# Batch 0's k sums from matmuls of their own, and its kv by head pair, in a fused attention and GEGLU kernel

## Chip, cores, metric

One core of a Trainium2 chip. The metric is the device time of one execution in microseconds (us). The profile gives a span, which runs from the first to the last instruction that it counts and is mostly 1.8 us shorter than the time. Engines: PE is TensorE, DVE is VectorE, ACT is ScalarE, POOL is GpSimd, SP is SyncE.

## The reference

```python
q_s = exp(q - max(q, -1)); q_s /= sum(q_s, -1)        # per token, over head_dim
k_s = exp(k - max(k, 2));  k_s /= sum(k_s, 2)         # per channel, over the sequence
kv  = einsum('bhsd,bhse->bhde', k_s, v)
x   = einsum('bhsd,bhde->bhse', q_s, kv)              # 8 batches, 8 heads, 576 tokens, 64 wide
out = (gelu(x @ w_gate) * (x @ w_val)) @ w_out        # x as [4608, 512]; d_ff = 1536
```

The kernel doesn't divide exp(k) by its sums; it divides kv by them, since the sum over the sequence is a factor of each row of kv.

## The kernel before

The FFN of all batches fills PE from 16 us on. The change touches what comes ahead of it for batch 0. The parts concerned, with cuts marked:

```python
def kv_mm(b, g, j):                       # one head pair; column D of v16 holds ones
    ...
    for n in range(NC):
        nc.tensor.matmul(st[(b, "pskv", g)][:, j, :], ek_b[b % 2][:, n, hp * P:(hp + 1) * P],
                         v16_b[b % 2][:, n, 2 * hp:2 * hp + 2, 0:VW], ...)     # VW = 65, N = 130

def kv_norm(b, g):                        # two head pairs
    nc.vector.reciprocal(out=rck, in_=pskv[:, :, D])
    for j in range(2):
        nc.vector.scalar_tensor_tensor(out=kv_sb, in0=pskv[:, j, ...], scalar=rck[:, j:j + 1], in1=mask, ...)

# the start, batch 0
norm_pair(0, 1, 1, ("dve", "pool")); evac_t0("dve")
warm_pe(11)
cast_v(0, 0, 2, "dve"); cast_v(0, 2, 4, "act"); cast_v(0, 6, 8, "dve"); cast_v(0, 4, 6, "act")
...                                       # loads of batches 1 and 2
kv_mm(0, 0, 0); kv_mm(0, 0, 1); kv_norm(0, 0)
unit_t(0, 1, "dve")                       # eight transposes of q and their copy
kv_mm(0, 1, 1)
unit_x(0, 0, "act", True)                 # x matmul of pair 0, copied by ACT to xt
kv_mm(0, 1, 0)
unit_x(0, 1, "act", True)
kv_norm(0, 1)
...
# first FFN block (two tiles together), x of pairs 2 and 3 in it
go(0, (0, 1)); xs(); go(1, (0, 1)); go(0, (2,)); go(1, (2,)); ...
```

Names in the profile's lines: ek and eq are exp(k) and exp(q), pskv is the product kv as PE writes it and kv_sb its normalised copy, pst are the transposes of eq and eqt their copy, psx the x matmuls and xt their copy, psg and psv the gate and value matmuls of the FFN, ht their product, psy the matmuls with w_out, pswarm the filler matmuls of PE (warm_pe), whose result isn't used. pks are the k sums.

The softmax here doesn't subtract the row's maximum and nothing guards it: scores larger than these inputs give would overflow.

Of the kernel before, what the change touches and what calls it, by code (L numbers as in the profile page):

```python
# [9 lines left out]
f32 = mybir.dt.float32  # L10
f16 = mybir.dt.float16
ACTF = mybir.ActivationFunctionType
ALU = mybir.AluOpType
# [5 lines left out]
def kernel(  # L19
# [10 lines left out]
    nc = tc.nc  # L30

    B, H, S, D = q.shape
    C = H * D
    F = moe_w_gate.shape[1]
    P = 128
    HP = H // 2
# [6 lines left out]
    NC = NM + 1  # L43
    MAIN = NM * P
    REM = S - MAIN
    VW = D + 1
# [4 lines left out]
    const = ctx.enter_context(tc.tile_pool(name="const", bufs=1))  # L51
    wpool = ctx.enter_context(tc.tile_pool(name="wpool", bufs=1))
    wstp = ctx.enter_context(tc.tile_pool(name="wstp", bufs=6))
    att = ctx.enter_context(tc.tile_pool(name="att", bufs=2))
# [3 lines left out]
    ps_big = ctx.enter_context(tc.tile_pool(name="ps_big", bufs=6, space=bass.MemoryType.PSUM))  # L58
    ps_att = ctx.enter_context(tc.tile_pool(name="ps_att", bufs=2, space=bass.MemoryType.PSUM))
# [4 lines left out]
    warm = const.tile([P, 512], f16)  # L64
    ident = const.tile([P, P], f16)
    mask = const.tile([P, 2, D], f32)
    tiny = const.tile([P, 80], f32)
    ek_b, eq_b, v16_b = [], [], []
    for i in range(2):
        ek_b.append(const.tile([P, NC, C], f16, name=f"ek{i}"))  # L70
# [9 lines left out]
    nc.vector.memset(ld_b["k"][0][:, :, 0:D], -1e30)  # L80
    nc.vector.memset(ld_b["v"][0][:, :, 0:D], 0.0)
    nc.vector.memset(tiny, 0.0)
    nc.vector.memset(mask, 0.0)
    nc.vector.memset(mask[0:64, 0, :], 1.0)
    nc.vector.memset(mask[64:128, 1, :], 1.0)
# [67 lines left out]
    def cast_v(b, h0, h1, eng="pool"):  # L153
        if eng == "pool" and h1 - h0 > 2:
            for h in range(h0, h1, 2):
                cast_v(b, h, h + 2)
            return
        copy_on(eng, v16_b[b % 2][:, :, h0:h1, 0:D].rearrange("p n h d -> p h n d"),
                tiles[("v", b)][:, h0:h1, :].rearrange("p h (n d) -> p h n d", d=D))
# [45 lines left out]

    def kv_mm(b, g, j):
        if (b, "pskv", g) not in st:
            pool, tag = (ps_big, "mm") if (b, g) == (0, 1) else (ps_att, "att")
            st[(b, "pskv", g)] = pool.tile([P, 2, 2 * VW], f32, name="pskv", tag=tag)
        hp = 2 * g + j  # L210
        for n in range(NC):
            nc.tensor.matmul(  # L212
                st[(b, "pskv", g)][:, j, :], ek_b[b % 2][:, n, hp * P:(hp + 1) * P],
                v16_b[b % 2][:, n, 2 * hp:2 * hp + 2, 0:VW],
                start=(n == 0), stop=(n == NC - 1))

    def kv_norm(b, g):
        pskv = st[(b, "pskv", g)]
        rck = att.tile([P, 2], f32, name="rck", tag="rck")
        nc.vector.reciprocal(out=rck, in_=pskv[:, :, D])  # L220
        for j in range(2):
            kv_sb = att.tile([P, 2, D], f16, name="kv_sb", tag="kv", bufs=12)
            nc.vector.scalar_tensor_tensor(
                out=kv_sb,
                in0=pskv[:, j, :].rearrange("p (h e) -> p h e", e=VW)[:, :, 0:D],
                scalar=rck[:, j:j + 1], in1=mask, op0=ALU.mult, op1=ALU.mult)
            st[(b, "kv", 2 * g + j)] = kv_sb

    def unit_kv(b, g):
        kv_mm(b, g, 0)  # L230
# [9 lines left out]
    def unit_t(b, g, eng="dve"):  # L240
        eqt = get_eqt(b)
        pst = ps_att.tile([P, 2, MAIN], f16, name="pst", tag="att")
        for j in range(2):
            hp = 2 * g + j
            for n in range(NM):
                nc.tensor.transpose(  # L246
                    pst[:, j, n * P:(n + 1) * P],
                    eq_b[b % 2][:, n + 1, hp * P:(hp + 1) * P], ident)
        st["evac_t"] = lambda eng: copy_on(eng, eqt[:, 2 * g:2 * g + 2, 0:MAIN], pst)
        if eng:  # L250
            st["evac_t"](eng)
# [49 lines left out]
    def unit_x(b, hp, eng="act", big=False):  # L301
        xt = get_xt(b)
        psx = (ps_big if big else ps_att).tile([P, MAIN], f32, name="psx",
                                               tag="mm" if big else "att")
        nc.tensor.matmul(psx, st[(b, "kv", hp)].rearrange("p h e -> p (h e)"),  # L305
                         xq(b, hp), start=True, stop=True)
        copy_on(eng, xt[:, hp, :], psx)
# [10 lines left out]
    def warm_pe(n):  # L318
        ps = pswarm
        for _ in range(n):  # L320
            nc.tensor.matmul(ps, ident, warm, start=True, stop=True)  # L321
# [5 lines left out]
    def mm_gv(ps, w, xt, fi, cis):  # L327
        for ci in cis:
            nc.tensor.matmul(ps, w[:, ci, fi * P:(fi + 1) * P], xt[:, ci, :],  # L329
                             start=(ci == 0), stop=(ci == HP - 1))  # L330
# [16 lines left out]
    def ffn_first(xt, after, between):  # L347

        ps = []
        for fi in range(len(after)):  # L350
            psg = ps_big.tile([P, 512], f32, name="psg", tag="mm")
            psv = ps_big.tile([P, 512], f32, name="psv", tag="mm")
            if fi == 0:
                for ci in range(2):
                    mm_gv(psg, wg_sb, xt, fi, [ci])
                    mm_gv(psv, wv_sb, xt, fi, [ci])
            else:
                mm_gv(psg, wg_sb, xt, fi, range(0, 2))
                for f in between[fi]:
                    f()  # L360
                mm_gv(psv, wv_sb, xt, fi, range(0, 2))
            ps.append((psg, psv))
            for f in after[fi]:
                f()
        for fi, (psg, psv) in enumerate(ps):
            mm_gv(psg, wg_sb, xt, fi, [2])
            mm_gv(psv, wv_sb, xt, fi, [2])
        hts = []
        for fi, (psg, psv) in enumerate(ps):
            mm_gv(psg, wg_sb, xt, fi, [3])  # L370
            mm_gv(psv, wv_sb, xt, fi, [3])
            hts.append(gate(psg, psv))
        return hts

    def ffn_first0(xt, xs):

        ps = {}
        for fi in range(2):
            for nm in ("g", "v"):
                ps[(nm, fi)] = ps_big.tile([P, 512], f32, name="ps" + nm, tag="mm")  # L380

        def go(fi, cis):
            for ci in cis:
                mm_gv(ps[("g", fi)], wg_sb, xt, fi, [ci])
                mm_gv(ps[("v", fi)], wv_sb, xt, fi, [ci])

        go(0, (0, 1))
        xs()
        go(1, (0, 1))
        go(0, (2,))  # L390
        go(1, (2,))
        hts = []
        for fi in range(2):
            go(fi, (3,))
            hts.append(gate(ps[("g", fi)], ps[("v", fi)]))
        return hts
# [85 lines left out]
    evac_t0 = st["evac_t"]  # L482
    norm_pair(0, 1, 1, ("dve", "pool"))
    evac_t0("dve")
    warm_pe(11)
    cast_v(0, 0, 2, "dve")
    cast_v(0, 2, 4, "act")
    cast_v(0, 6, 8, "dve")
    cast_v(0, 4, 6, "act")
    for h0 in (0, 4):  # L490
        load(k, "k", 1, h0, h0 + 4, 0)
        load(v, "v", 1, h0, h0 + 4, 0)
    load_batch(2, ((q, "q"), (k, "k")))
    nc.sync.dma_start(out=q0r, in_=q[0].rearrange("h (m n) d -> m h (n d)", n=NT)[:, :, 0:D])
    kv_mm(0, 0, 0)
    kv_mm(0, 0, 1)
    kv_norm(0, 0)
    unit_t(0, 1, "dve")
    kv_mm(0, 1, 1)
    cast_w("wg", 0, "pool")  # L500
    cast_w("wv", 0, "pool")
    unit_x(0, 0, "act", True)
    kv_mm(0, 1, 0)
    unit_x(0, 1, "act", True)
    kv_norm(0, 1)
    preload(ACTF.Gelu)
    for c in range(1, NW):
        cast_w("wg", c)
# [22 lines left out]
    first1 = ([[L(unit_kv, 1, 1), L(unit_t, 1, 1)], [], [L(unit_x, 1, 3, "dve")]],  # L531
              [[], [], [L(unit_x, 1, 2, "act")]])

    def x_upper():
        unit_x(0, 2, "dve")
        unit_x(0, 3, "act")


    at(1, FI, 2, L(unit_trem, 1))
# [52 lines left out]
    for b in order:  # L592
        xt = get_xt(b) if b < B else xtr
        hts = []
        fi0 = 0
        if b < 2:
            hts = ffn_first0(xt, x_upper) if b == 0 else ffn_first(xt, *first1)
            fi0 = len(hts)
            ride(b, FI, fi0 - 1)
        for fi in range(fi0, NFI):  # L600
            hts.append(ffn_fi(xt, fi))
            ride(b, FI, fi)
        if b == 0:
            psys = []
            for ns in range(4):
                psys.append(ps_big.tile([P, C], f32, name="psy", tag="mm"))
                mm_out(psys[ns], hts, ns, range(0, NFI // 2))
                ride(b, NS, ns)
            for ns in range(4):
                cut = 10 if ns == 3 else NFI  # L610
                mm_out(psys[ns], hts, ns, range(NFI // 2, cut))
                ride(b, NS, 14 + ns)
                mm_out(psys[ns], hts, ns, range(cut, NFI))
                evac(b, ns, psys[ns], "act" if ns == 3 else "dve")
                ride(b, NS, 4 + ns)
        else:
            for ns in range(4):
                if b == order[-1] and ns == 3:
                    last_rows(b, hts, ns)
                    break  # L620
                psy = ps_big.tile([P, C], f32, name="psy", tag="mm")
                mm_out(psy, hts, ns, range(NFI // 2))
                ride(b, NS, 10 + ns)
                mm_out(psy, hts, ns, range(NFI // 2, NFI))
                evac(b, ns, psy)
                ride(b, NS, ns)
# [30 lines left out]
```

## Time and profile before

| what | before |
|---|---|
| time, median of 3 runs (lowest to highest) | 319.98 us (319.97 to 320.21) |
| span of the profiled run | 318.5 us |
| PE busy | 98% |
| first psg (first useful FFN matmul) | 15.96 us |
| first psg of the third FFN tile | 19.91 us |

From the third FFN tile on, the FFN's own matmuls follow each other without a break that the change touches, so **the start of the third tile** is the mark that I use for the start. Its line in the timeline of the kernel before (columns: start us, duration us, engine, line, operation, output<-inputs, count):

```profile
19.91 1.03 PE L329 MATMUL psg<-xt,wg_sb 128*128 128x512 f16 x4
```

### The profile page before, as it was taken

How to read it: one execution, taken by the hardware profiler on the slowest of the kernel's cores; microseconds unless marked ns; L12 is line 12 of the kernel's file. 1: busy time of each engine (PE TensorE's matmuls, PEld its weight loads, DVE VectorE, ACT ScalarE, POOL GpSimd, SP SyncE). 2: the span in 40 equal slices, each digit the busy share in tenths (PEclk: the TensorE clock that was granted, in tenths of full speed). 3: DMA queues.
4: the chain of work that ended last, by engine and by line, in shares of the span. 5: the costliest groups of instructions: out<-in, count | busy, mean ns of one | idle time of the engine just before them, and what ended most of it. 6: DMA issues, size and time to landing. Idle time of an engine off the chain costs nothing.

```text
span 318.5 us, 4464 instructions
## 1 busy us (share of the span) xinstructions
PE 312.0 (98%) x1645; PEld 148.9 (47%) x1645; DVE 194.7 (61%) x341; ACT 139.7 (44%) x179; POOL 44.8 (14%) x59
## 2 busy tenths in 40 slices
PE   8899999999999999999999999999999999999995
PEld 3444454445445444544444444444444444444444
DVE  3944386698898469847784679457952434233331
ACT  3653565989433663256433753384331233113300
POOL 2657551330003000110003000300000000000000
PEclk9999999999999999999999999999999999999999
DMA  6999999940196117811592139303011110040002
GB/s 232 372 383 395 400 388 385 393 156 0 68 313 241 44 66 246 297 52 66 167 363 66 53 117 385 94 15 132 0 54 32 74 60 0 20 108 6 0 35 99
DMA packets 42342, 50.76 MB, mean 159 GB/s; under 512 B 3408, under 2 KB 38096, under 8 KB 42320
## 3 DMA queue, kind: packets, MB, share of 16 engines
q1 hardware_dynamic: 40592, 48.84, 44.2%
q10 hardware_dynamic: 1728, 1.64, 1.6%
q8 instruction: 13, 0.21, 0.3%
q14 instruction: 9, 0.07, 0.1%
HBM read 37.75 MB, written 9.44 MB: 148 GB/s over the span
## 4 chain that ended last, share of the span: by engine, by line
PE 88%; DMA 4%; ACT 3%; DVE 2%; issue 1%; POOL 0%; ACTq 0%; DVEq 0%; POOLq 0%
PE psy L403 28%; PE psg L329 26%; PE psv L329 26%; PE pskv L212 3%; DMA out_dram<-yo 2%; PE psx L305 2%; DMA qt<-in_q_dram 2%; PE psl L424 1%; PE pswarm L321 1%; DVE rq L165 1%; DVE ht L336 1%; ACT eq L148 1%; PE pst L246 1%; ACT xt L128 1%; POOL eq L184 0%
## 5 line engine op out<-in xcount | busy, mean ns | idle before, releaser
L334 ACT ACTIVATE gl<-psg 128x512 f32<-128x512 f32 x108 | 63.9, 598 | 128.5 <-PE psg L329 125.5
L336 DVE SCALAR_TENSOR_TENSOR ht<-psv,gl 128x512 f16<-128x512 f32 x108 | 72.9, 682 | 63.6 <-PE psv L329 63.0
L329 PE MATMUL psg<-xt,wg_sb 128*128 128x512 f16 x384 | 100.6, 379 | 0.3 <-ACT xt L128 0.2
L329 PE MATMUL psv<-xt,wv_sb 128*128 128x512 f16 x384 | 100.7, 379 | 0.0
L403 PE MATMUL psy<-wo_sb,ht 128*128 128x512 f16 x420 | 95.6, 379 | 0.0
L329 PEld LDWEIGHTS <-wv_sb 128*128 128x128 f16 x432 | 42.2, 98 | 51.8 <-issue 1.0
L329 PEld LDWEIGHTS <-wg_sb 128*128 128x128 f16 x432 | 41.5, 98 | 47.1 <-issue 0.4
L403 PEld LDWEIGHTS <-ht 128*128 128x128 f16 x420 | 40.5, 98 | 47.1 <-DVE ht L336 0.2
L452 DVE TENSOR_SCALAR yo<-psy 128x512 f32<-128x512 f32 x30 | 20.6, 689 | 31.2 <-PE psy L403 31.2
L126 POOL CAST v<-vt 128x640 f16<-128x640 f32 x26 | 18.8, 763 | 138.9 <-DMA vt<-in_v_dram 100.4
L165 DVE TENSOR_REDUCE rq<-eq 128x10 f32<-128x640 f16 x28 | 22.7, 812 | 5.1 <-ACT eq L148 4.6
L184 DVE TENSOR_TENSOR eq<-eq,rrq 128x640 f16<-128x640 f16 (+1 forms) x29 | 23.6, 815 | 0.3
L148 ACT ACTIVATE ek<-kt 128x1280 f16<-128x1280 f32 (+1 forms) x11 | 19.1, 1746 | 3.5 <-DMA kt<-in_k_dram 3.4
L148 ACT ACTIVATE eq<-qt 128x2560 f16<-128x2560 f32 (+2 forms) x10 | 18.4, 1863 | 2.3 <-DMA qt<-in_q_dram 2.3
L271 DVE STREAM_TRANSPOSE et<-eq 128x640 f16<-128x640 f16 x20 | 16.9, 846 | 0.7
L128 ACT CAST xt<-psx 128x512 f16<-128x512 f32 x17 | 9.3, 587 | 13.8 <-PE psx L305 13.8
L329 PE MATMUL psg<-xtr,wg_sb 128*128 128x512 f16 x48 | 12.3, 379 | 0.0
L329 PE MATMUL psv<-xtr,wv_sb 128*128 128x512 f16 x48 | 12.3, 379 | 0.0
L212 PEld LDWEIGHTS <-ek 128*128 128x128 f16 x160 | 10.5, 97 | 3.4
L212 PE MATMUL pskv<-v,ek 128*128 128x130 f16 x160 | 12.0, 220 | 0.0
L321 PE MATMUL pswarm<-warm,ident 128*128 128x512 f16 x41 | 10.6, 420 | 1.4 <-POOL ident masks.py:199 1.4
L130 DVE CAST xt<-psx 128x512 f16<-128x512 f32 x15 | 9.7, 682 | 2.1 <-PE psx L305 2.1
(60 smaller groups left out, 129.3 us busy)
## 6 DMA issues: line engine op xcount, KB each, us to landing
out_dram<-yo SPq DMA_DIRECT2D x14, 512.0 KB, 3.3
kt<-in_k_dram SPq DMA_DIRECT2D x7, 640.0 KB, 7.8
vt<-in_v_dram SPq DMA_DIRECT2D x7, 640.0 KB, 8.1
qt<-in_q_dram SPq DMA_DIRECT2D x7, 640.0 KB, 5.2
qt<-in_q_dram SPq DMA_DIRECT2D x8, 512.0 KB, 5.9
eqt<-et SPq DMA_DIRECT2D x80, 40.0 KB, 1.9
wost<-in_moe_w_out_dram SPq DMA_DIRECT2D x6, 512.0 KB, 7.9
kt<-in_k_dram SPq DMA_DIRECT2D x6, 512.0 KB, 7.9
```

The lines of the kernel that those rows point to most:

```text
L126: nc.gpsimd.tensor_copy(out=dst, in_=src)
L148: nc.scalar.activation(out=dst[:, n0:NC, h0 * D:h1 * D].rearrange("p n (h d) -> p h n d", d=D), in_=tiles[(nm, b)][:, h0:h1, n0 * D:NC * D ...
L165: nc.vector.reduce_sum(rq, e, axis=mybir.AxisListType.X)
L184: (nc.gpsimd if eng == "pool" else nc.vector).tensor_tensor(out=e, in0=e, in1=rrq.unsqueeze(-1).to_broadcast((P, n, 2, D)), op=ALU.mult)
L212: nc.tensor.matmul(st[(b, "pskv", g)][:, j, :], ek_b[b % 2][:, n, hp * P:(hp + 1) * P], v16_b[b % 2][:, n, 2 * hp:2 * hp + 2, 0:VW], start ...
L271: nc.vector.transpose(out=et[:, :, hp].rearrange("p c (n i) -> p n c i", i=32), in_=eq_b[b % 2][:, :, hp * P:(hp + 1) * P].rearrange("p n ...
L321: nc.tensor.matmul(ps, ident, warm, start=True, stop=True)
L329: nc.tensor.matmul(ps, w[:, ci, fi * P:(fi + 1) * P], xt[:, ci, :], start=(ci == 0), stop=(ci == HP - 1))
L334: nc.scalar.activation(out=gl, in_=psg, func=ACTF.Gelu)
L336: nc.vector.scalar_tensor_tensor(out=ht, in0=psv, scalar=_H_SCALE, in1=gl, op0=ALU.mult, op1=ALU.mult)
L403: nc.tensor.matmul(psy, hts[fi][:, ns * P:(ns + 1) * P], wo_sb[:, fi, :], start=(fi == 0), stop=(fi == NFI - 1))
L452: nc.vector.tensor_scalar(out=yo, in0=psy, scalar1=1.0 / _H_SCALE, scalar2=None, op0=ALU.mult)
```

## The change

The intent: let the sums of exp(k) be ready before v arrives, so that the reciprocal is off the chain from v to the first FFN matmul; let pair 0 go on without pair 1; and take PE's filler matmuls out of the way. The diff:

```diff
--- before.py
+++ after.py
@@ -64,7 +64,8 @@
     warm = const.tile([P, 512], f16)
     ident = const.tile([P, P], f16)
     mask = const.tile([P, 2, D], f32)
-    tiny = const.tile([P, 80], f32)
+    ones = const.tile([P, 1], f16)
+    tiny = const.tile([P, 72], f32)
     ek_b, eq_b, v16_b = [], [], []
     for i in range(2):
         ek_b.append(const.tile([P, NC, C], f16, name=f"ek{i}"))
@@ -80,6 +81,7 @@
     nc.vector.memset(ld_b["k"][0][:, :, 0:D], -1e30)
     nc.vector.memset(ld_b["v"][0][:, :, 0:D], 0.0)
     nc.vector.memset(tiny, 0.0)
+    nc.vector.memset(ones, 1.0)
     nc.vector.memset(mask, 0.0)
     nc.vector.memset(mask[0:64, 0, :], 1.0)
     nc.vector.memset(mask[64:128, 1, :], 1.0)
@@ -205,8 +207,7 @@
 
     def kv_mm(b, g, j):
         if (b, "pskv", g) not in st:
-            pool, tag = (ps_big, "mm") if (b, g) == (0, 1) else (ps_att, "att")
-            st[(b, "pskv", g)] = pool.tile([P, 2, 2 * VW], f32, name="pskv", tag=tag)
+            st[(b, "pskv", g)] = ps_att.tile([P, 2, 2 * VW], f32, name="pskv", tag="att")
         hp = 2 * g + j
         for n in range(NC):
             nc.tensor.matmul(
@@ -225,6 +226,34 @@
                 in0=pskv[:, j, :].rearrange("p (h e) -> p h e", e=VW)[:, :, 0:D],
                 scalar=rck[:, j:j + 1], in1=mask, op0=ALU.mult, op1=ALU.mult)
             st[(b, "kv", 2 * g + j)] = kv_sb
+
+
+    def ksum_mm(hps):
+        if "pks" not in st:
+            st["pks"] = ps_big.tile([P, HP], f32, name="pks", tag="mm")
+        for hp in hps:
+            for n in range(NC):
+                nc.tensor.matmul(st["pks"][:, hp:hp + 1], ek_b[0][:, n, hp * P:(hp + 1) * P], ones,
+                                 start=(n == 0), stop=(n == NC - 1))
+
+    def ksum_rec():
+        st["rck0"] = att.tile([P, HP], f32, name="rck0", tag="rck0", bufs=1)
+        nc.vector.reciprocal(out=st["rck0"], in_=st["pks"])
+
+    def kv0_mm(hp):
+        pool, tag = (ps_att, "att") if hp == 0 else (ps_big, "mm")
+        st[("pskv0", hp)] = pool.tile([P, P], f32, name="pskv0", tag=tag)
+        for n in range(NC):
+            nc.tensor.matmul(
+                st[("pskv0", hp)], ek_b[0][:, n, hp * P:(hp + 1) * P],
+                v16_b[0][:, n, 2 * hp:2 * hp + 2, 0:D], start=(n == 0), stop=(n == NC - 1))
+
+    def kv0_norm(hp):
+        kv_sb = att.tile([P, 2, D], f16, name="kv_sb", tag="kv", bufs=12)
+        nc.vector.scalar_tensor_tensor(
+            out=kv_sb, in0=st[("pskv0", hp)].rearrange("p (h e) -> p h e", e=D),
+            scalar=st["rck0"][:, hp:hp + 1], in1=mask, op0=ALU.mult, op1=ALU.mult)
+        st[(0, "kv", hp)] = kv_sb
 
     def unit_kv(b, g):
         kv_mm(b, g, 0)
@@ -385,8 +414,12 @@
                 mm_gv(ps[("v", fi)], wv_sb, xt, fi, [ci])
 
         go(0, (0, 1))
-        xs()
-        go(1, (0, 1))
+        xs[0]()
+        for ci in range(2):
+            mm_gv(ps[("g", 1)], wg_sb, xt, 1, [ci])
+        xs[1]()
+        for ci in range(2):
+            mm_gv(ps[("v", 1)], wv_sb, xt, 1, [ci])
         go(0, (2,))
         go(1, (2,))
         hts = []
@@ -482,27 +515,31 @@
     evac_t0 = st["evac_t"]
     norm_pair(0, 1, 1, ("dve", "pool"))
     evac_t0("dve")
-    warm_pe(11)
+    warm_pe(2)
+    ksum_mm((0, 1))
+    warm_pe(2)
+    ksum_mm((2, 3))
     cast_v(0, 0, 2, "dve")
     cast_v(0, 2, 4, "act")
+    ksum_rec()
+    cast_v(0, 4, 6, "act")
+    kv0_mm(0)
+    kv0_mm(1)
+    kv0_norm(0)
+    kv0_norm(1)
     cast_v(0, 6, 8, "dve")
-    cast_v(0, 4, 6, "act")
     for h0 in (0, 4):
         load(k, "k", 1, h0, h0 + 4, 0)
         load(v, "v", 1, h0, h0 + 4, 0)
     load_batch(2, ((q, "q"), (k, "k")))
     nc.sync.dma_start(out=q0r, in_=q[0].rearrange("h (m n) d -> m h (n d)", n=NT)[:, :, 0:D])
-    kv_mm(0, 0, 0)
-    kv_mm(0, 0, 1)
-    kv_norm(0, 0)
-    unit_t(0, 1, "dve")
-    kv_mm(0, 1, 1)
     cast_w("wg", 0, "pool")
     cast_w("wv", 0, "pool")
     unit_x(0, 0, "act", True)
-    kv_mm(0, 1, 0)
+    kv0_mm(2)
     unit_x(0, 1, "act", True)
-    kv_norm(0, 1)
+    kv0_norm(2)
+    unit_t(0, 1, "dve")
     preload(ACTF.Gelu)
     for c in range(1, NW):
         cast_w("wg", c)
@@ -531,9 +568,10 @@
     first1 = ([[L(unit_kv, 1, 1), L(unit_t, 1, 1)], [], [L(unit_x, 1, 3, "dve")]],
               [[], [], [L(unit_x, 1, 2, "act")]])
 
-    def x_upper():
+    def x_upper0():
+        kv0_mm(3)
+        kv0_norm(3)
         unit_x(0, 2, "dve")
-        unit_x(0, 3, "act")
 
 
     at(1, FI, 2, L(unit_trem, 1))
@@ -594,7 +632,7 @@
         hts = []
         fi0 = 0
         if b < 2:
-            hts = ffn_first0(xt, x_upper) if b == 0 else ffn_first(xt, *first1)
+            hts = ffn_first0(xt, (x_upper0, L(unit_x, 0, 3, "act"))) if b == 0 else ffn_first(xt, *first1)
             fi0 = len(hts)
             ride(b, FI, fi0 - 1)
         for fi in range(fi0, NFI):
```

## The prediction

> **What bounds the kernel now.** I read the page's busy row and tenths first, then the waits of TensorE (PE), then the timeline of the first 20 us, because the diff touches only batch 0's start.
>
> ```profile
> PE 312.0 (98%) x1645; PEld 148.9 (47%) x1645; DVE 194.7 (61%) x341; ACT 139.7 (44%) x179; POOL 44.8 (14%) x59
> ```
>
> PE is busy 98% of 318.5 us. The waits of PE over the whole execution are only these four:
>
> ```profile
> PE pswarm L321 <- POOL ident masks.py:199: 1.4, 1, 1.4
> PE pst L246 <- DVE eq L184: 0.7, 1, 0.7
> PE pst L246 <- POOL eq L184: 0.4, 1, 0.4
> PE psg L329 <- ACT xt L128: 0.2, 1, 0.2
> ```
>
> All lie before 16.0 us. From there PE has a full queue, so the end is the moment of the first useful FFN matmul plus the PE work after it. But "busy" before 16 us is partly filler (pswarm), and the chain there runs through other engines. The timeline (start us, duration us, engine, line):
>
> ```profile
> 10.12 2.43 ACT L148 ACTIVATE ek<-kt 128x1280 f16<-128x1280 f32 x2 [1.51 <-DMA kt<-in_k_dram]
> ...
> 11.13 2.54 PE L321 MATMUL pswarm<-warm,ident 128*128 128x512 f16 x11
> ...
> 12.66 1.36 ACT L128 CAST v<-vt 128x640 f16<-128x640 f32 x2
> 12.68 1.05 DVE L130 CAST v<-vt 128x640 f16<-128x640 f32 x2
> ...
> 13.51 0.74 PE L212 MATMUL pskv<-v,ek 128*128 128x130 f16 x10
> ...
> 14.08 0.61 PE L246 MATMUL pst<-ident,eq 128*128 128x128 f16 x8
> 14.28 0.17 DVE L220 RECIPROCAL rck<-pskv 128x2 f32<-128x2 f32 x1 [0.55 <-PE pskv L212]
> 14.49 0.61 DVE L223 SCALAR_TENSOR_TENSOR kv_sb<-pskv,rck,mask 128x128 f16<-128x128 f32 x2
> ...
> 14.90 0.39 PE L305 MATMUL psx<-eqt,kv_sb 128*128 128x512 f16 x1
> ...
> 15.32 1.09 ACT L128 CAST xt<-psx 128x512 f16<-128x512 f32 x2 [1.30 <-PE psx L305]
> ...
> 15.96 0.38 PE L329 MATMUL psg<-xt,wg_sb 128*128 128x512 f16 x1 [0.17 <-ACT xt L128]
> ```
>
> The reader should see one thread: v cast, kv matmuls, reciprocal, normalisation, x matmul, x copy, first psg at 15.96. The eleven warm matmuls end issuing at 13.51 (11 x 0.216 = 2.38 after 11.13), while the first v cast is done by about 13.25: PE itself holds kv up by 0.25. Then ten kv matmuls are waited for as one, and the reciprocal sits on the path.
>
> **What the Trainium skill says.** "TensorE: Matmul & The Clock Gate", Back-to-back issue gap, gives N/2.4 + 2.5 ns warm. The trace agrees: eleven N=512 matmuls at 0.216 us each, and N=130 ones at 0.057 (0.57 of the chain for ten). The same section puts a floor of 25 ns under a small N, or 62 ns if the sequencer decodes. No N=1 matmul is in this trace; since each of the 20 new ones brings its own 128-column weight load, and such pairs go at 0.057 here, I take 0.057. The same page, The HAM clock gate, says the PE clock halves after about 3.4 us of idling. The trace shows the start of it: the first warm weight loads stand 0.43 us apart, those after 4.30 us 0.21; idling of 0.66 and 0.43 before the transposes didn't bring the slow rate back. "PSUM — Partial Sum Buffer", The four PSUM rules, says a first matmul of a group clears the flags of its whole bank, so groups of one bank must not be open together: the four k sums of one bank run one after the other, so the result should be right.
>
> **The change, part by part.** Removed: seven warm matmuls (11 become 4), one of two reciprocals, the ones column of each kv matmul (N 130 to 128, 20 x under 1 ns: nothing). Added: 20 k-sum matmuls of N=1 (20 x 0.057 = 1.14 us of PE) in the time the filler had. PE there was idle in truth, so neither is worth anything by itself. Moved: kv of pair 2 between the two x matmuls; the second transposes behind them; kv of pair 3 and its normalisation behind the first four FFN matmuls; the two upper x matmuls into the first FFN block; DVE's cast of heads 6-7 behind two normalisations. ACT, POOL and SP keep their order.
>
> I work out the new times from durations above. Three latencies come from start-to-start gaps before: normalisation to the x matmul 14.90 - 14.49 = 0.41 (its own duration, 0.35, plus 0.05); x matmul to ACT copy 15.32 - 14.90 = 0.42; copy to psg 15.96 - 15.32 = 0.64. A matmul's result is seen about 0.26 after its start (last of ten kv at 14.02, reciprocal at 14.28).
>
> 1. ek's second half ends 12.55, so the last ten k sums run 12.60 to 13.17 and the reciprocal (DVE) about 13.37 to 13.54, right after DVE's only v cast before it, whose heads 0-1 are ready at 13.29.
> 2. kv of pair 0: 13.29, five at 0.057, last at 13.52, seen 13.78. Normalisation at 13.78 instead of 14.49; it no longer waits for pair 1 nor for its own reciprocal.
> 3. x of pair 0: 13.78 + 0.41 = 14.19 instead of 14.90. ACT copies it at 14.61; first psg possible at 15.25.
> 4. kv of pair 1: 13.57 to 13.86, seen 14.06; normalised, usable 14.46. kv of pair 2 14.40 to 14.69, then x of pair 1 at 14.69, its copy at 15.13 (behind the first, 0.52 apart) and usable 15.77.
> 5. The eight transposes take PE from 14.90 to 15.35, past 15.25: **first psg at 15.35**, 0.61 earlier than 15.96. The xt of pair 1 at 15.77 fits the third matmul.
> 6. From there PE has, up to its third FFN tile: 16 FFN matmuls (16 x 0.2155 = 3.45), two x (0.43) and, new, kv of pair 3 (0.28): 4.16, so 15.35 + 4.16 = 19.51. Before: 15.96 + 3.45 + 0.43 = 19.84, and 0.07 of gap made it 19.91. Check of the new waits: pair 3's kv is seen at 16.70, normalised, usable 17.10 and wanted at 17.14; DVE's xt of pair 2 runs after that, 16.96 to 17.65, wanted at 17.79. Both fit by less than 0.1.
>
> Sum: 0.61 - 0.28 + 0.07 = **0.40 us** earlier, 319.98 - 0.40 = 319.58, so I say **319.6 us**. The number of PE matmuls after that point is the same, and none is shortened.
>
> **Rivals.** (a) The gain is lost later to the DMA queue, since the loads of the weights and of batch 1 keep their times. For it: until 58 us the queue moves some 390 GB/s and other engines wait on it:
>
> ```profile
> 38.57 1.04 POOL L126 CAST wo_sb<-wost 128x1024 f16<-128x1024 f32 x1 [3.25 <-DMA wost<-in_moe_w_out_dram]
> ...
> 41.15 1.57 POOL L126 CAST wo_sb<-wost 128x1024 f16<-128x1024 f32 x1 [0.21 <-DMA wost<-in_moe_w_out_dram]
> ...
> 47.29 1.39 POOL L126 CAST v<-vt 128x640 f16<-128x640 f32 x2 [1.25 <-DMA vt<-in_v_dram]
> ```
>
> The last w_out piece is ready at 42.72; its first matmul is the 29th of those that start at 37.18, thus 37.18 + 28 x 0.2155 = 43.21 before and 42.81 after. It fits by 0.09, and v's cast (done 48.7) by 0.9 before the kv at 49.7. If it didn't fit, the whole 0.4 would go and the time be 319.9 to 320.0. Against it: PE waits for none of these before. (b) PE's clock falls back. In 11.1 to 14.5 its array now works about half the time, and N=1 matmuls may not count as activity. If the slow rate came back for one stretch of 3.4 us from 14.5 on, half of it, 1.7 us, would be lost, less the 0.4: about 321.3. Against: idle pieces stay under 0.4 us, and the four warm matmuls kept are spread for this. I give it 7%. (c) The k sums go slower than 0.057, say at 0.10: the last ten would end at 13.6, pair 0 starts 0.3 later, and only 0.1 remains: 319.9. (d) DVE is late on pair 3 or its xt, by 0.1 to 0.3, as step 6 has so little slack: 319.7 to 319.9. Nothing speaks for a gain beyond 0.6, as the transposes, the k load and the v load keep their times.
>
> **Range and chances.** The three runs before spread 0.24 us, as much as half the gain, so the sign itself is not certain. Mostly (a), (c), (d) shrink it; errors of my latencies go both ways by 0.2. I take 319.2 to 320.2 for 8 in 10. A change of 2% would be 6.4 us, and the whole start up to the first psg is 16 us with the loads unchanged in it: within 2% 0.99, faster 0.005, slower 0.005.
>
> **What would show it.** In the timeline of the kernel after: k sums about 0.057 apart, done by 13.2; one reciprocal near 13.4; the first psx near 14.2, the first psg near 15.35, and the third tile's psg near 19.5. In the waits of PE: small entries (0.1 to 0.3) for v, kv_sb and perhaps xt before 15.4, none after 20. I am wrong in the mechanism if the k sums end after 13.4, if the N=512 matmuls after 14 us stand 0.43 apart, if PE waits on wo_sb near 42.8, or if the third tile starts at 19.5 and the end isn't earlier.

## The result

| | before | after |
|---|---|---|
| time, median of 6 runs in the same rounds | 320.18 us (319.97 to 320.40) | 320.00 us (319.52 to 320.21) |
| span of the profiled run | 318.46 | 317.89 |
| first psg | 15.96 | 15.44 |
| third tile | 19.91 | 19.60 |
| third tile to end of span | 298.54 | 298.29 |

(The spans to 0.01 us are from the first and last record of each trace; the profile prints 318.5 and 317.9.) The ratio is 0.9993, 95% interval 0.998 to 1.0006. (A ratio is the mean time of one kernel's runs over that of the other's of the same rounds, so not quite the ratio of the medians.) The interval doesn't even settle the sign.

The waits of PE in the kernel after (who waited on whom, us in total, times, longest):

```profile
PE pswarm L350 <- POOL ident masks.py:199: 1.4, 1, 1.4
PE pskv L247 <- DVE v L132: 0.5, 1, 0.5
PE pst L275 <- POOL eq L186: 0.4, 1, 0.4
PE psx L334 <- DVE kv_sb L253: 0.2, 1, 0.2
```

PE now waits for v's cast instead of being late for it: the filler is out of the way, and the reciprocal is no entry. The timeline of the same stretch:

```profile
12.49 0.40 PE L236 MATMUL pks<-ones,ek 128*128 128x1 f16 x10
...
12.65 0.67 DVE L132 CAST v<-vt 128x640 f16<-128x640 f32 x1
...
13.25 0.17 DVE L241 RECIPROCAL rck<-pks 128x4 f32<-128x4 f32 x1
...
13.38 0.72 PE L247 MATMUL pskv<-v,ek 128*128 128x128 f16 x10 [0.49 <-DVE v L132]
...
13.86 0.63 DVE L253 SCALAR_TENSOR_TENSOR kv_sb<-pskv,rck,mask 128x128 f16<-128x128 f32 x2 [0.44 <-PE pskv L247]
...
14.27 0.39 PE L334 MATMUL psx<-eqt,kv_sb 128*128 128x512 f16 x1 [0.17 <-DVE kv_sb L253]
...
15.44 0.38 PE L358 MATMUL psg<-xt,wg_sb 128*128 128x512 f16 x1
...
19.60 1.03 PE L358 MATMUL psg<-xt,wg_sb 128*128 128x512 f16 x4
```

The reader should see the k sums done before v's cast, the reciprocal done in the shadow of kv, and the normalisation at 13.86 instead of 14.49. The third tile is 0.31 us earlier. But the two spans differ by 0.57, and the mean times by only 0.23 (320.155 - 319.925). Neither is 0.31, so two things had to be found: where the profiled runs part by another 0.26, and why single runs scatter over 0.4 to 0.7 us.

The first is found by comparing marks along the span. Output copies at 48 us stand 0.32 apart, those at 76 us 0.57, and from there on all stand 0.57 apart. In between, near 70 us, lies this. The timeline of the kernel before (POOL, DVE, PE):

```profile
69.96 1.98 POOL L126 CAST v<-vt 128x640 f16<-128x640 f32 x2
70.18 1.17 DVE L184 TENSOR_TENSOR eq<-eq,rrq 128x640 f16<-128x640 f16 x1
70.94 0.86 PE L246 MATMUL pst<-ident,eq 128*128 128x128 f16 x8
```

And of the kernel after:

```profile
69.86 0.83 DVE L186 TENSOR_TENSOR eq<-eq,rrq 128x640 f16<-128x640 f16 x1
69.96 1.98 POOL L128 CAST v<-vt 128x640 f16<-128x640 f32 x2
70.63 0.61 PE L275 MATMUL pst<-ident,eq 128*128 128x128 f16 x8
```

The DVE line is the last normalising multiply of batch 2's q; the transposes of PE wait for it, without showing as a wait, because the first four of the eight run and the group is merged. POOL casts batch 3's v from 68.6 us on in both kernels, as the load lands at a fixed time. In the kernel before the multiply starts in the middle of a cast and takes 1.17 us; in the kernel after it is 0.32 earlier, starts 0.10 ahead of a cast, and takes 0.83. The Trainium skill, "SBUF — State Buffer", Who interferes with whom, says that a DVE instruction with two SBUF inputs and a POOL instruction that reads SBUF share one port pair, and that whoever issues first holds it for its whole length while the other blocks. The trace agrees: where the multiply is first, the cast behind it is the long one (its next starts at 71.22, 1.26 us later, against 0.66 undisturbed). Where the cast is first, it sets the end of the multiply: in the kernel before the multiply starts at 70.18 and ends at 71.35, and in a second profile of the kernel after, in which the whole start was late (next section), it starts at 70.39, 0.21 later, in the middle of a cast again, and ends at 71.37; the spans of these two are 318.46 and 318.47 us. So inside a cast a start that is earlier by some tenths can be lost again.

### The profile page after: what moved, and what is told of

Same layout as the page of the kernel before. It is cut to its first block, busy times and chain, and to the rows that moved or that the text cites. A ratio compares the mean times of both kernels' runs of the same rounds, so it can differ in the third digit from the quotient of the medians. Undisturbed runs are those within 1.5% of the kernel's fastest.

```text
span 317.9 us, 4491 instructions
## 1 busy us (share of the span) xinstructions
PE 311.6 (98%) x1658; PEld 148.8 (47%) x1658; DVE 194.1 (61%) x341; ACT 139.8 (44%) x179; POOL 44.7 (14%) x59
## 4 chain that ended last, share of the span: by engine, by line
PE 90%; DMA 4%; ACT 3%; DVE 2%; issue 1%; ACTq 0%
PE psy L436 28%; PE psg L358 27%; PE psv L358 27%; PE pskv L213 2%; DMA out_dram<-yo 2%; PE psx L334 2%; DMA qt<-in_q_dram 2%; PE psl L457 1%; DVE rq L177 1%; ACT eq L150 1%; PE pst L275 1%; DVE eq L186 0%; ACT L363 0%; ACT L150 0%; ACT L353 0%
## 5 line engine op out<-in xcount | busy, mean ns | idle before, releaser
L350 PE MATMUL pswarm<-warm,ident 128*128 128x512 f16 x34 | 9.9, 452 | 1.4 <-POOL ident masks.py:199 1.4
L213 PEld LDWEIGHTS <-ek 128*128 128x128 f16 x140 | 9.1, 97 | 3.1
```

Source lines behind the costliest of these rows:

```text
L350: nc.tensor.matmul(ps, ident, warm, start=True, stop=True)
```

## The experiments

**Theory.** The change is worth a fixed 0.3 us at the start. What a single run shows besides is chance: when the first q load lands, and how the multiply near 70 us meets POOL's casts. **Rivals:** the whole 0.57 us belongs to the change; or the gain comes from one part alone (filler, k sums, the place of pair 3's kv) and the rest does nothing.

Eleven kernels ran, all correct, in three groups of one chip each. The kernel before ran in each group: median 320.20 (320.03 to 320.35, 9 runs), 320.16 (320.02 to 320.55, 9 runs), 320.19 (320.05 to 320.46, 7 runs).

### The kernel after again

No edit.

> The kernel after once more, unchanged, to separate its fixed gain from scatter. Theory (start gain 0.31 us, rest is a collision of VectorE's last normalising multiply of batch 2 with GpSimd's v casts near 70 us that falls differently from run to run): the third FFN tile's first psg at 19.60 us again within 0.03, the mean time 0.2 to 0.4 us below the kernel before of the same rounds, and the runs of both spread over 0.3 to 0.7 us. Rival (the gain is the full 0.57 us that the two profiles differ by): mean 0.57 below, each run.

Measured: median 320.11 us (319.54 to 320.29, 5 runs), ratio 0.9991, interval 0.9978 to 1.0005; means 319.97 against 320.18. The third tile came at 20.13 instead of 19.60: a miss of the absolute number, because the whole start was late. The first exp of q, which waits for the load, began at 7.14 us in this run and at 6.60 in the first profile. Counted from the start of v's first cast the third tile comes after 6.94 us, and 6.95 in the first profile. So I measure from there in what follows: 7.23 for the kernel before (19.91 - 12.68). The spread, and the mean gain of 0.21, are as expected; the rival's 0.57 each time is out.

### POOL's casts held back, first try

```diff
+    held = const.tile([P, 1], f16)
+    def pool_hold():
+        nc.gpsimd.tensor_copy(out=held, in_=st["ht"][:, 0:1])     # ht of batch 1's last tile
-    ... L(exp_rem0), L(cast_v, 3, 0, H))
+    ... L(exp_rem0), L(pool_hold), L(cast_v, 3, 0, H))
```

Applied to the kernel before and to the kernel after:

> The kernel before, with GpSimd's casts of batch 3's v held back until the last ht of batch 1 is written, so that they can't meet the multiply near 70 us. Theory: the multiply takes 0.83 instead of 1.17 us, PE's pause of some 0.25 us ahead of the second half of the transposes near 71 us is gone, the third tile stays at 19.91, the mean time falls by 0.1 to 0.3 us against the kernel before and the runs spread less (under 0.25 us). Rival (the scatter comes from elsewhere): same mean and same spread as the kernel before.

> The kernel after with the same hold. Theory: third tile at 19.60, time 0.31 us (0.1%) below that of the kernel before with the hold, spread under 0.25 us, and little or no gain over the kernel after where that one had no collision. Rival (the difference of the two profiles is all start gain): 0.57 us below the kernel before with the hold.

Measured: 323.34 us (ratio 1.01, interval 1.0086 to 1.0113) and 323.14 us (1.0095, 1.0081 to 1.0109). Both failed as tests: the loads from 8 to 56 us ran at 331 to 374 GB/s instead of 373 to 400, and PE waited 1.5 us for POOL's casts of w_out, which wait for their loads. In the waits of the kernel before with the hold:

```profile
PE psy L408 <- POOL wo_sb L127: 1.5, 2, 1.1
```

The multiply near 70 us did take 0.83 and 0.82. I had added a small tile behind the first three and so moved the addresses of everything after it. The change under study adds such a tile too (ones), and takes 8 columns off another (tiny, 80 to 72), which I had passed over as housekeeping.

### The kernel after without that compensation

```diff
-    tiny = const.tile([P, 72], f32)
+    tiny = const.tile([P, 80], f32)
```

> The kernel after with tiny at its old 80 columns, so that the new ones tile moves every later tile by its own size. Theory (the first hold's 3 us came from moved addresses): loads at about 345 instead of 390 GB/s between 16 and 56 us, PE waits for casts of weights, time near 323. Rival (that cost was the hold's): 320.0.

Measured: 323.18 us (322.82 to 323.36, 4 runs), ratio 1.0091, interval 1.0076 to 1.0106. So the eight columns are worth 3 us, ten times the change's gain. Stretches of the kernel after (busy time of PE, PEld, DVE, ACT, POOL with instruction counts; granted clock; DMA share; GB/s):

```profile
16.00:24.00 8.00, 8.00 (x43) 3.73 (x41) 3.93 (x7) 4.14 (x7) 4.84 (x6) 1.00 1.09 383
24.00:32.00 8.00, 8.00 (x39) 3.64 (x38) 2.83 (x6) 2.98 (x5) 6.14 (x7) 1.00 1.08 396
...
40.00:48.00 8.00, 8.00 (x52) 4.05 (x49) 7.02 (x15) 4.82 (x4) 4.26 (x4) 1.00 1.08 386
```

And of this kernel:

```profile
16.00:24.00 8.00, 8.00 (x48) 3.71 (x46) 3.75 (x7) 4.92 (x9) 4.51 (x6) 1.00 1.10 344
24.00:32.00 8.00, 7.53 (x36) 3.25 (x35) 3.03 (x5) 2.39 (x4) 5.37 (x6) 1.00 1.09 351
...
40.00:48.00 8.00, 6.54 (x32) 2.80 (x30) 4.50 (x9) 4.99 (x4) 3.47 (x3) 1.00 1.07 367
```

The DMA engines are as busy (share 1.07 to 1.10), they only move less; and PE, full in the one, has holes of 0.47 and 1.46 us in the other. The loads carry the same bytes in the same pieces; only where they land in SBUF has moved. The Trainium skill, "DMA: Bandwidth & Descriptors", How a descriptor splits into AXI transactions, tells of pieces that start off a 256-byte boundary and cost extra beats. Something like it may be at work, but that is not shown: the page speaks of reads, and here the written end moved. I neither looked up the addresses nor varied the shift, so the mechanism and the rule stay open.

### POOL's casts held back, addresses kept

As above, with tiny smaller by 8 columns more (72 in the kernel before, 64 in the kernel after).

> The kernel before with the hold on GpSimd's casts of batch 3's v, and the small tile that the hold writes paid for by 8 columns of tiny, so that every later tile lies where it did. Theory (the 3 us that the first hold cost came from the moved addresses, since its loads ran at some 345 instead of 390 GB/s): loads back at 380 to 395 GB/s, time back near 320. Theory of the collision: the multiply near 70 us takes 0.83 us and the time is 0.1 to 0.3 us below the kernel before, 319.9 to 320.1, spread down to what the first q load's landing gives (0.5 us between fast and slow landings). Rival (the hold itself costs 3 us): 323.3 again.

> The kernel after with the same hold at unmoved addresses. Theory: multiply 0.83 us, the time 0.3 us below the before kernel with the hold, about 319.6 to 319.8. Rival (the start gain is worth the 0.57 us of the two first profiles): 0.57 below.

Measured: 319.95 us (319.89 to 320.06, 5 runs; ratio 0.9991, interval 0.9979 to 1.0004) and 319.70 us (319.69 to 319.93, 5 runs; 0.9985, 0.9972 to 0.9999). The hold itself costs nothing. The spread fell from 0.53 (before, nine runs of the same rounds; 0.32 over nine runs of the first group) to 0.17 over five runs, and for the kernel after from 0.69 and 0.75 to 0.24. Part of this may be luck: the landing of the first load alone moved the start by up to 0.5 us from profile to profile (first exp at 6.60 to 7.14), as the expectation says, and these five and five runs show nothing of that size. The difference of the two held kernels is 0.21 in the means (319.97 - 319.76), 0.22 in the mean spans; worked out from the scatter of these ten runs, the 95% interval of the 0.21 is about 0.07 to 0.34. The timeline of the kernel before with the hold:

```profile
70.26 0.82 DVE L185 TENSOR_TENSOR eq<-eq,rrq 128x640 f16<-128x640 f16 x1
75.34 0.19 POOL L343 COPY held<-ht 128x1 f16<-128x1 f16 x1 [14.29 <-DVE ht L337]
```

The multiply is at 0.82 with POOL silent until 75 us. The rest of the span from the third tile is 298.3 in both (318.3 - 20.00 and 317.9 - 19.62). In the kernel after with the hold the multiply starts at 69.88 and takes 0.82. So the extra 0.26 us of the first pair was the collision, which the two profiles met differently, and not a second gain of the change.

### One part at a time

**Less filler alone**, in the kernel before:

```diff
-    warm_pe(11)
+    warm_pe(9)
```

> The kernel before with 9 instead of 11 warm matmuls ahead of kv, nothing else. Theory (the filler itself holds kv up): kv starts when v's first cast is done, 0.73 us after that cast's start instead of 0.83, and the third tile comes 0.10 us earlier, 7.13 instead of 7.23 us after the start of v's first cast. Rival 1 (the reciprocal and the second pair pace it): 7.23. Rival 2 (fewer warm matmuls let PE's clock fall): matmuls of N=512 stand 0.43 us apart after 14 us and the time rises by over 1 us.

Measured: 320.11 us (319.92 to 320.27, 4 runs), ratio 0.9996, interval 0.9981 to 1.0011. Its timeline:

```profile
12.71 1.08 DVE L130 CAST v<-vt 128x640 f16<-128x640 f32 x2
13.44 0.73 PE L212 MATMUL pskv<-v,ek 128*128 128x130 f16 x10 [0.15 <-ACT v L128]
...
19.84 1.03 PE L329 MATMUL psg<-xt,wg_sb 128*128 128x512 f16 x4
```

kv starts 0.73 after the cast's start and the third tile 7.13 after it, both as expected. FFN matmuls after it stand 0.22 apart, so the clock didn't fall. Here the multiply near 70 us took 1.28, and the mean time is 0.12 below the kernel before, well inside the scatter.

**No k sums** in the kernel after; each pair has the ones column and a reciprocal of its own:

```diff
-    ksum_mm((0, 1)); warm_pe(2); ksum_mm((2, 3)); ...; ksum_rec()
+    warm_pe(2)
 def kv0_norm(hp):
+    nc.vector.reciprocal(out=rck, in_=st[("pskv0", hp)][:, D:D + 1])
```

> The kernel after without the k sums: kv by pair, each with the ones column (N=130) and a reciprocal of its own. Theory (the reciprocal sits on the path for 0.17 + 0.04 us): first psx 0.21 us after that of the kernel after relative to the end of v's first cast, third tile 0.2 to 0.3 us later (about 19.8 to 19.9 if the first q lands as in the first profiles), so that little of the gain is left. Rival (the k sums buy nothing since the second pair's matmuls or the transposes set the pace): third tile as in the kernel after.

Measured: 320.21 us (320.08 to 320.70, 5 runs), ratio 1.0001, interval 0.9989 to 1.0014.

```profile
12.61 0.65 DVE L132 CAST v<-vt 128x640 f16<-128x640 f32 x1
...
13.80 0.17 DVE L254 RECIPROCAL rck<-pskv 128x1 f32<-128x1 f32 x1 [0.54 <-PE pskv L247]
14.01 0.35 DVE L255 SCALAR_TENSOR_TENSOR kv_sb<-pskv,rck,mask 128x128 f16<-128x128 f32 x1
...
14.41 0.39 PE L336 MATMUL psx<-eqt,kv_sb 128*128 128x512 f16 x1 [0.36 <-DVE kv_sb L255]
...
19.94 0.81 PE L360 MATMUL psg<-xt,wg_sb 128*128 128x512 f16 x3
```

The first psx comes 1.80 us after the cast's start instead of 1.62, as expected. The third tile comes after 7.33, 0.38 later than in the kernel after and even 0.10 later than before: more than I expected, since pair 3's reciprocal sits on the path a second time, in the FFN block, where psx of pair 3 comes at 17.55 instead of 17.23. So the split into pairs without the k sums loses, and the gain needs the k sums. K sums without the split into pairs were not run.

**Pair 3's kv ahead of the FFN** in the kernel after:

```diff
     unit_x(0, 1, "act", True)
+    kv0_mm(3)
     kv0_norm(2)
+    kv0_norm(3)
 def x_upper0():
-    kv0_mm(3)
-    kv0_norm(3)
```

> The kernel after with kv of pair 3 and its normalisation ahead of the FFN, before the second transposes, instead of behind the first four FFN matmuls. Theory (PE would wait there for VectorE's cast of heads 6-7, done some 2.55 us after the start of v's first cast): first psg near 3.3 us and third tile near 7.2 us after the start of v's first cast, against 2.79 and 6.95 in the kernel after, so the whole gain is gone. Rival (the place of these five matmuls doesn't matter, PE has them to do in any case): 6.95 again.

Measured: 320.16 us (320.08 to 320.39, 4 runs), ratio 0.9997, interval 0.9980 to 1.0013.

```profile
12.96 0.67 DVE L132 CAST v<-vt 128x640 f16<-128x640 f32 x1
...
14.71 0.77 DVE L132 CAST v<-vt 128x640 f16<-128x640 f32 x1
...
15.54 0.45 PE L247 MATMUL pskv<-v,ek 128*128 128x128 f16 x5
15.83 0.61 PE L275 MATMUL pst<-ident,eq 128*128 128x128 f16 x8
...
16.27 0.38 PE L358 MATMUL psg<-xt,wg_sb 128*128 128x512 f16 x1
...
20.24 1.03 PE L358 MATMUL psg<-xt,wg_sb 128*128 128x512 f16 x4
```

The first psg is 3.31 after the cast's start and the third tile 7.28: as late as before the change. PE stood waiting for heads 6-7, whose cast ended at 15.48. The same matmuls inside the dense FFN block cost only their own 0.28.

### A rearranged start

PE still waits 0.5 us for v, and the second transposes, which need no v, stand on the path. So: transposes into that wait, heads 6-7 cast by ACT, and with v ready early, all kv ahead of the FFN.

```diff
     cast_v(0, 4, 6, "act")
+    cast_v(0, 6, 8, "act")
+    unit_t(0, 1, None)
     kv0_mm(0)
     ...
-    cast_v(0, 6, 8, "dve")
+    evac_t1("dve")
     ...
     kv0_mm(2)
     unit_x(0, 1, "act", True)
+    kv0_mm(3)
     kv0_norm(2)
-    unit_t(0, 1, "dve")
+    kv0_norm(3)
```

> The kernel after, with the eight second transposes moved into PE's wait for v (12.7 to 13.3 us), v's heads 6-7 cast by ACT instead of VectorE, and kv of pair 3 ahead of the FFN again. Theory (PE order decides once the first xt is there): first psg at 15.34 us, limited by ACT's copy of xt, third tile at 15.34 + 16 x 0.2155 + 2 x 0.2155 = 19.22, so 0.38 us below the kernel after and 0.69 below the kernel before at that point; time about 319.5. Rival (ACT gets too late by the third cast): first psg at 15.5 to 15.7, third tile at 19.4 to 19.6, no gain over the kernel after.

Measured: 320.37 us (319.69 to 320.78, 5 runs), ratio 1.0005, interval 0.9993 to 1.0018: no gain in the time, though the start did what it should.

```profile
15.35 0.38 PE L358 MATMUL psg<-xt,wg_sb 128*128 128x512 f16 x1
...
19.29 1.03 PE L358 MATMUL psg<-xt,wg_sb 128*128 128x512 f16 x4
...
69.56 1.36 DVE L186 TENSOR_TENSOR eq<-eq,rrq 128x640 f16<-128x640 f16 x1
```

The third tile is 6.61 us after the start of v's cast, 0.34 better than the kernel after (0.05 of the expected 0.38 went to a gap between the first pairs of FFN matmuls). But the multiply took 1.36 us, and by 75.7 us this kernel was 0.13 behind the kernel after. The larger loss is another: its time was 2.2 to 2.4 us longer than its span, where the other kernels have 1.7 to 1.9 in all but two runs. In the mean span of its runs it gained: 318.04 against 318.38 for the kernel before in the same rounds. The part outside lies beyond what the profile records, and I can't explain it. With the hold:

> The rearranged start (transposes in the wait for v, v's heads 6-7 on ACT, all kv ahead of the FFN) with the hold. Theory (the gain of 0.31 us that its third tile shows was eaten by a multiply of 1.36 us near 70 us): multiply 0.83 us, span 0.3 us below the kernel after with the hold and 0.6 below the kernel before with the hold. Rival (something later absorbs an earlier start): same span as the kernel after with the hold. Open: whether the time outside the span is again 2.3 instead of 1.8 us.

Measured: 319.72 us (319.55 to 320.07, 5 runs), ratio 0.9985, interval 0.9973 to 0.9998. The multiply took 0.83, the third tile came 6.62 after the cast's start, and the mean span of the runs is 317.86, against 317.96 for the kernel after with the hold and 318.18 for the kernel before with the hold: 0.10 and 0.32 less, where 0.3 and 0.6 were expected, a miss. One of its five runs again had 2.3 us outside the span, the others 1.8. In the mean time it is level with the kernel after with the hold (319.77 and 319.76); both beat the kernel before of the same rounds by 0.5 us, and the kernel after, which ran in other rounds, by 0.2. The profiled run had a late q load (7.11 us), which hides the start's gain in that span; the first load of the other four runs isn't on record, so whether late loads explain the whole miss stays open.

### All profiled runs side by side

| kernel | start of v's first cast | from there to the third tile | third tile to end | the multiply near 70 us | span |
|---|---|---|---|---|---|
| before | 12.68 | 7.23 | 298.54 | 1.17 | 318.46 |
| before, 9 warm | 12.71 | 7.13 | 298.64 | 1.28 | 318.48 |
| before, hold | 12.76 | 7.24 | 298.28 | 0.82 | 318.28 |
| after | 12.65 | 6.95 | 298.29 | 0.83 | 317.89 |
| after again | 13.19 | 6.94 | 298.34 | 0.98 | 318.47 |
| after, hold | 12.69 | 6.93 | 298.28 | 0.82 | 317.90 |
| after, own reciprocals | 12.61 | 7.33 | 298.35 | 0.97 | 318.29 |
| after, pair 3 early | 12.96 | 7.28 | 298.34 | 0.98 | 318.58 |
| rearranged | 12.68 | 6.61 | 298.72 | 1.36 | 318.02 |
| rearranged, hold | 13.17 | 6.62 | 298.27 | 0.83 | 318.07 |

Each span is the sum of its first three numbers, within 0.01. The first follows the landing of the first load, which is chance; the second is the kernel's structure and repeats to 0.02 us; and the third rises with the multiply's duration: 298.27 to 298.29 at 0.82 or 0.83 us, 298.34 or 298.35 at 0.97 or 0.98, and up to 298.72 at 1.36. (The kernels with moved addresses are left out.)

## Why the prediction was right

The mechanism was right, and the size too large: 0.40 us forecast; 0.29 in the marks of the traces (7.235 - 6.94, the means of two and of three profiles), 0.21 to 0.23 in the mean times of three pairs. The time of 320.0 lies in the range, but that is weak support, since the kernel before at 320.18 lies in it too: the three runs that the forecast started from had a median of 319.98, 0.2 below that of the six. The times of the two pairs without the hold don't tell 0.2 from nothing; the traces and the held pair do. The sign of being wrong that was named last, an earlier third tile with no earlier end, didn't come: in the two first profiles both are earlier.

- **Steps 1 to 3, v to first psx.** Forecast 14.19, measured 14.27. The order of the waits was as told, with 0.5 us for v instead of 0.1 to 0.3. The missing 0.08 is one term: I took 0.566 us for v's first cast, the mean of DVE's two casts before. They were 0.652 and 0.481, and the first is the one on the path (0.67 after). The grouped row hid it, and with it the filler's part: PE held kv up by 0.10 us, as the kernel with 9 warm matmuls shows, and not by 0.25. The kernel with tiny at 80 shows why the casts differ: there v lands at 13.63, after POOL's multiply of q is over (it ends at 13.32), and the same cast takes 0.50; in the kernel after that multiply runs to 12.98, across the cast's start at 12.65. First the kernel after, then the one with tiny at 80:

```profile
11.49 1.49 POOL L186 TENSOR_TENSOR eq<-eq,rrq 128x512 f16<-128x512 f16 x1 [0.66 <-DVE rrq L179]
...
12.65 0.67 DVE L132 CAST v<-vt 128x640 f16<-128x640 f32 x1
```

```profile
13.63 0.50 DVE L132 CAST v<-vt 128x640 f16<-128x640 f32 x1 [0.62 <-DMA vt<-in_v_dram]
```

The cast has one SBUF input, but is of the kinds that "SBUF — State Buffer", Who interferes with whom, names as able to take both ports. The other profiles agree: the first cast took 0.65 to 0.67 us in all ten of the table, where POOL's multiply runs across its start, and 0.50 in the three kernels with moved addresses, where it doesn't.

- **Step 5, first psg.** Forecast 15.35, measured 15.44: the same 0.09, nothing added.
- **Step 6.** Forecast 4.16 us from first psg to third tile, measured 19.60 - 15.44 = 4.16. Both tight waits fitted.
- **The k sums** were cheaper than I took them: ten in 0.39, thus (0.39 - 0.16)/9 = 0.025 us apart against my 0.057. They were off the path in either case; the kernel with own reciprocals shows that having them is worth 0.38.
- **Rival (a)**, loss to the DMA queue: not so at kept addresses; PE waits for no load. (Its slack for v's cast before kv was 49.7 - 48.7 = 1.0, not 0.9.) It was right about how thin the slack is: at moved addresses just these casts of w_out stop PE.
- **Rival (b)**, the clock: FFN matmuls stand 0.216 apart after 15 us in all runs. Not so.
- **Rival (c) and (d)**: not so. DVE's lateness came, but as the 0.09 in v's cast.
- **What I hadn't seen**: the collision near 70 us. The prediction said "none is shortened" of the work after the start, and counted the scatter of the runs as noise. It decides how much of an earlier start arrives at the end: 298.29 or 298.34 us after the third tile in two profiles of the same kernel. How much of the scatter of the runs is the collision and how much the first load is not settled. Nor did I see that the eight columns of tiny belong to the change.

## What to carry to other kernels

When a gain of a few tenths doesn't show, compare the same marks along both traces: here the start gained 0.3, and a DVE multiply meeting a POOL cast gave back or added up to 0.4 depending on when the chain arrived. A sum that needs only one operand can be had before the other operand arrives, and then its reciprocal is off the path; splitting work into smaller pieces without that put the reciprocal on the path twice and lost. A new small tile can move every buffer behind it: after any change of tiles, look at the loads' GB/s before believing the time.

## What the Trainium skill lacked or had wrong

- "TensorE: Matmul & The Clock Gate", Back-to-back issue gap: its floor of about 25 ns for small N held, even where each N=1 matmul brings its own 128-column weight load (ten in 0.39 us, 25 ns apart); the page gives that floor for matmuls and doesn't say that such weight loads keep up with it.
- "SBUF — State Buffer", Who interferes with whom: the exclusive lock held as told (multiply 0.82 us free, up to 1.36 behind a cast; cast 1.26 instead of 0.66 behind the multiply). It lacks that this can differ between two executions of one kernel: multiply 0.83 us in one, 0.98 in the other.
- "DMA: Bandwidth & Descriptors", How a descriptor splits into AXI transactions: it tells of starts off a 256-byte boundary for reads. No page has the cost of a shifted destination in SBUF: 344 to 351 instead of 383 to 396 GB/s and 3 us of the time, for one small tile.
- No page tells of the difference between the span and the device time as these runs have it, 1.7 to 1.9 us in most and 2.2 to 2.4 in some.
